# Attention and routed experts on one core: a new order of TensorE's steps in units 0 to 2 of a pair of heads

## The chip, the cores and the metric

One core of a Trainium2 chip runs one program. The metric is the device time of one execution in microseconds (us); several executions are timed and their median is taken. TensorE is called PE in the profile, its weight loads PEld, VectorE DVE, ScalarE ACT, GpSimd POOL and SyncE SP.

## What is computed

Attention over 8 batches, 8 heads, 576 positions and head size 64, with a position bias from a small network; its output feeds a layer of eight experts, of which each token takes one. All of it is float32.

```python
scores = scale * np.matmul(q, k.transpose(0, 1, 3, 2)) + bias
attn = np.exp(scores - np.max(scores, axis=-1, keepdims=True))
attn = attn / (np.sum(attn, axis=-1, keepdims=True) + 1e-09)
x = np.matmul(attn, v)                     # then (token, 512)
e_idx = argmax(x @ w_gate + modality_bias[modality_id]); gate_w = softmax(...)[e_idx]
out[mask] = gate_w[mask, None] * (np.maximum(x[mask] @ w1[e], 0.0) @ w2[e])
```

## The kernel before

There are three stages: the bias table (up to about 66 us in the profiled execution), attention (to about 665 us), and the experts. The change lies in attention.

Attention works through 32 pairs of heads, two heads of one batch at a time, in a loop over n. Each pair has five units u of work, one for each chunk c of 128 rows of scores (the fifth chunk holds the last 64 rows of both heads). The program sets each engine's queue itself: an engine's instructions stand in its queue in the order in which `attention` writes them, and no planner reorders them. The order in a unit is a line of letters in `ORDER`. Work of three pairs is interleaved: scores and exponentials of pair n, products with v of pair n-1, preparation of q and k of pair n+1, loading for pair n+2.

- S (twice a unit) is `scores`, L430: four matmuls of 288 columns (six in unit 4) into one of two score banks `sps`. DVE then adds the bias, writes to `Eb` and takes the minimum `mn` (L445). `e` and `f` are the exponentials on ACT (L459) of the unit's first and second S.
- T and t are `etrans`, parts 1 and 0: four 128x128 transposes each into the bank `eps[1]` or `eps[0]`, which is copied out to `eT`, by ACT or DVE as the list `ON_ACT` says (L315, L317). They belong to the chunk w: in units 0 and 1 to chunks 3 and 4 of pair n-1, in units 2 to 4 to chunks 0 to 2 of pair n. For chunk 4, t is L479 and T is the narrow form, L484: two products of 64 columns, one into each half of the partitions, copied by ACT into the last 64 columns of `rT`.
- R is `rtrans` (L501): four transposes of the left-over columns `rem`, which POOL has copied (C, `compact`), to one of the two small banks `xps`; ACT copies it into `rT`, columns 0 to 511.
- a, A, b, c are `av`, the products with v (L517), for the output's columns 0 to 287 (a then A) and 288 to 575 (b then c). Each is four calls with a 64-column weight that writes one half of the partitions; each call is two matmuls in the profile. A and c end with the remainder (L527, weight `vrem`, moving `rT`), and ACT copies the sum to `xT` (named `xTb` in the profile, L315). The bank is taken in a or b and held in `self.avps`.
- 0, 1, 2, 3, 4 are `prep`: 1 and 0 transpose q (L379), 4 the last rows of q and k (L384), 2 and 3 k (L379), into a small bank, from which DVE or ACT copies into `QT` (L319) or `KT`. W is `swap`, two DMAs on SP's queue (L403, L404) which write `QT` with its halves exchanged; K is `heads`, small DMAs.
- q and k are splits on POOL; L and V are loads on SP's queue; D and Z store and scatter for the routing. X and B are the next step of the routing of the batch before, on PE (X) or elsewhere (B), if one is due; `route_next` picks it. In X are the logits (L771, L794), the ranks (L842) and five transposes of output rows (L866), whose copies to `xrb` ACT does.

The two small banks `xps` are shared by R, X, the products and the preparations. `xbank` hands them out in turn:

```python
def xbank(self):
    self.n_x += 1
    return self.xps[self.n_x % 2]
```

A bank's next writer waits for the copy out of it; the framework places this wait.

Of the kernel before, what the change touches and what calls it, by code (L numbers as in the profile page):

```python
# [22 lines left out]
S = 576  # L23
D = 64
# [43 lines left out]
def n_first(nb):  # L68

    return max(0, min(5, -(-(S * (nb - 2) - E * (TS - 1)) // TS)))  # L70
# [37 lines left out]
class Attn:  # L108
    def __init__(self, tc, io, out, dbg=None):
        self.tc, self.nc, self.io, self.out, self.dbg = tc, tc.nc, io, out, dbg  # L110
        self.B = io["q"].shape[0]
        self.n_tok = self.B * S
        self.n_pair = self.B * NP
        self.K = n_first(self.B)
        self.stores, self.scatters = [], []

# [187 lines left out]
        self.eps = [pp.tile([P, 4, P], F32, name=f"eps{k}") for k in range(2)]  # L304

    def xbank(self):
        self.n_x += 1
        return self.xps[self.n_x % 2]

    ON_ACT = ("av0", "av1", "e00", "e11", "e20", "e30", "e31", "e40", "e41", "prep2", "prep5", "rT", "xr")  # L310
# [193 lines left out]
    def av(self, n, half, part):  # L504

        nc = self.nc
        if half == 0 and part == 0:
            self.xT[n] = self.xTb[n // NP % 2][:, n % NP, :]
        if part == 0:
            self.avps = self.xbank()  # L510
        v = self.vmain[n]
        sl = slice(HS * half, HS * half + HS)
        ps = self.avps[:, 0:HS]
        for k in (0, 1) if part == 0 else (2, 3):
            for h in range(2):
                o = slice(64 * h, 64 * h + 64)
                nc.tensor.matmul(  # L517
                    ps[o, :],
                    v[:, h, k, :],
                    self.eT[:, h, k, sl],  # L520
                    start=k == 0,
                    stop=False,
                    tile_position=(0, 64 * h),
                    skip_group_check=True,
                )
        if part == 1:
            nc.tensor.matmul(ps, self.vrem[n % 2], self.rT[:, sl], start=False, stop=True, skip_group_check=True)  # L527
        if part == 1:
            self.take(f"av{half}", self.xT[n][:, sl], ps)
            if half == 1:  # L530
                del self.vmain[n]

    def first_steps(self, route):
# [40 lines left out]


    ORDER = (
# [5 lines left out]
    )  # L582
# [890 lines left out]
```

## Time and profile before

| what | value |
|---|---|
| median of 3 runs | 1154.85 us (1152.61 to 1155.16) |
| profiled execution, its own time | 1160.33 us |
| its span, first to last instruction | 1158.4 us |
| PE busy | 1121.5 us (97%) |
| DVE busy | 748.6 us (65%) |
| ACT busy | 731.8 us (63%) |
| POOL busy | 361.0 us (31%) |

A share is an average over the three stages, so the attention stage is read by windows. In a row of the timeline stand the start, the length, the engine, the line and the tiles; in square brackets the idle time ahead of it and what ended that. A row of windows has the stretch, its length, the busy time and count of PE, PEld, DVE, ACT and POOL, then the granted clock of PE as a share of full speed, the busy share of the DMA engines and GB/s. Ends of matmuls are modelled, and rows of matmuls in sequence overlap.

### The profile page before, as it was taken

The numbers are of one execution on the slowest core, as the hardware profiler recorded it, in microseconds if no ns is written. First come the engines' busy times: TensorE is split into PE (matmuls) and PEld (weight loads), VectorE is DVE, ScalarE is ACT, GpSimd is POOL, SyncE is SP. The second block draws the span as 40 slices with busy tenths as digits, with TensorE's granted clock in tenths as the row PEclk, the third lists the DMA queues.
The fourth block names the chain that finished last, engine by engine and source line by source line (L and its number), as shares of the span: only waits on it lengthen the run. The fifth ranks groups of instructions, "written<-read, shape, count | busy, mean of one in ns | idle before, by whom it ended". The sixth has DMA issues, their size and how long they took to land. (4 is left out here: it accounts for less than half of the span.)

```text
span 1158.4 us, 23054 instructions
## 1 busy us (share of the span) xinstructions
PE 1121.5 (97%) x8202; PEld 912.4 (79%) x8202; DVE 748.6 (65%) x1556; ACT 731.8 (63%) x1420; POOL 361.0 (31%) x514
## 2 busy tenths in 40 slices
PE   7989999999999999999999999999999999999997
PEld 3457877778777777877777769899999999999975
DVE  8965667676675766756668547584566455645576
ACT  7776767767676676776766646454555455545576
POOL 0013334435434444254352234412112222212122
PEclk9989999999999999999999989999999999999999
DMA  6984434635545544454463721211115115112370
GB/s 176 222 173 113 107 97 124 115 96 130 110 108 121 123 122 104 105 129 108 121 121 96 204 33 56 60 47 46 56 38 175 62 57 196 42 47 65 110 261 26
DMA packets 91456, 124.54 MB, mean 108 GB/s; under 512 B 35713, under 2 KB 60673, under 8 KB 91332
## 3 DMA queue, kind: packets, MB, share of 16 engines
q1 hardware_dynamic: 83236, 101.61, 34.8%
q0 software_dynamic: 8000, 21.35, 6.2%
q8 instruction: 68, 1.11, 0.5%
q14 instruction: 56, 0.46, 0.2%
q10 hardware_dynamic: 96, 0.00, 0.0%
HBM read 140.36 MB, written 19.90 MB: 138 GB/s over the span
## 5 line engine op out<-in xcount | busy, mean ns | idle before, releaser
L445 DVE CUSTOM_DVE_ANT_0 Eb<-sps,NBm 128x576 f32<-128x576 f32 x256 | 189.6, 754 | 160.0 <-PE sps L430 89.1
L459 ACT ACTIVATE Eb<-Eb,mn 128x576 f32<-128x576 f32 x288 | 221.4, 769 | 36.9 <-DVE mn L445 33.5
L430 PE MATMUL sps<-KT,QT 128*128 128x288 f32 x1152 | 220.4, 317 | 3.9 <-DMA QT<-QT 3.7
L430 PEld LDWEIGHTS sps<-KT,QT 128*128 128x128 f32 x1152 | 164.6, 190 | 9.0 <-issue 4.5
L1188 PE MATMUL p<-QT,w1hi 128*128 128x256 f32 x1152 | 162.2, 284 | 0.0
L473 PE MATMUL eps<-idf,Eb 128*128 128x128 f32 x1024 | 158.5, 281 | 0.6 <-DVE lgs L810 0.3
L517 PE MATMUL xps<-eT,vraw 128*64 128x288 f32 x1024 | 155.1, 425 | 1.5 <-DVE QT L1173 1.0
L1188 PEld LDWEIGHTS p<-QT,w1hi 128*128 128x128 f32 x1152 | 149.5, 192 | 2.2 <-ACT w1hi L1161 0.8
L473 PEld LDWEIGHTS eps<-idf,Eb 128*128 128x128 f32 x1024 | 113.9, 141 | 39.0 <-issue 29.3
L1191 DVE SCALAR_TENSOR_TENSOR hl<-p,hh 128x512 fp32r<-128x512 f32 x72 | 49.7, 690 | 141.5 <-ACT hh L1190 140.0
L1214 POOL DMA_INDIRECT out<-mo,idt x36 | 48.0, 1333 | 298.5 <-ACT mo L1213 262.4
L464 POOL COPY rem<-Eb 128x128 f32<-128x128 f32 x128 | 37.2, 291 | 318.8 <-ACT Eb L459 312.3
L1155 DVE TENSOR_TENSOR w2lo<-NBm,w2hi 128x1024 fp32r<-128x1024 f32 x84 | 102.3, 1224 | 24.8 <-ACT w2hi L1154 18.7
L1205 PE MATMUL p<-w2hi,hh 128*128 128x512 f32 x288 | 115.3, 400 | 0.0
L315 ACT ACTIVATE eT<-eps 128x512 f32<-128x512 f32 x192 | 110.6, 591 | 6.8 <-PE eps L473 5.9
L1205 PE MATMUL p<-w2hi,hl 128*128 128x512 f32 x288 | 113.7, 395 | 0.0
L1190 ACT ACTIVATE hh<-p 128x512 fp32r<-128x512 f32 x72 | 43.0, 597 | 111.5 <-PE p L1188 101.3
L315 ACT ACTIVATE xTb<-xps 128x288 f32<-128x288 f32 x64 | 26.3, 411 | 117.0 <-PE xps L527 114.4
L517 PEld LDWEIGHTS xps<-eT,vraw 128*64 128x64 f32 x1024 | 63.2, 138 | 46.1 <-issue 12.3
L1155 DVE TENSOR_TENSOR w1lo<-NBm,w1hi 128x1024 fp32r<-128x1024 f32 x84 | 97.7, 1225 | 0.2 <-ACT w1hi L1154 0.2
L1188 PE MATMUL p<-QT,w1lo 128*128 128x256 f32 x576 | 92.9, 284 | 1.0 <-DVE w1lo L1162 1.0
L1154 ACT CAST w2hi<-NBm 128x1024 fp32r<-128x1024 f32 x84 | 86.8, 1040 | 0.7 <-PEq L1318 0.7
(235 smaller groups left out, 1945.9 us busy)
## 6 DMA issues: line engine op xcount, KB each, us to landing
NBm<-moe_w SPq DMA_DIRECT2D x24, 2048.0 KB
NBm<-moe_w SPq DMA_DIRECT2D x46, 1024.0 KB
QT<-QT SPq DMA_DIRECT2D x64, 304.0 KB
NBm<-xTb SPq DMA_DIRECT2D x32, 288.0 KB
KH<-KT SPq DMA_DIRECT2D x64, 144.0 KB
qraw<-q SPq DMA_DIRECT2D x32, 256.0 KB
kraw<-k SPq DMA_DIRECT2D x32, 256.0 KB
vraw<-v SPq DMA_DIRECT2D x32, 256.0 KB
```

Source lines behind the costliest of these rows:

```text
L315: self.nc.scalar.activation(out, ps, AF.Copy, scale=scale)
L430: nc.tensor.matmul(ps[:, half, :], q, k[:, HS * half : HS * half + HS], start=i == 0, stop=i == len(terms) - 1, skip_group_check=True,)
L445: nc.vector.tensor_tensor_reduce(out=e.rearrange("p (t w) -> p t w", t=2), in0=ps, in1=nb.rearrange("p (t w) -> p t w", t=2), scale=1.0, s ...
L459: self.nc.scalar.activation(e, e, AF.Exp, bias=mn, scale=-1.0, accum_out=sm)
L473: nc.tensor.transpose(ps[:, k, :], e[:, part, P * k : P * k + P], self.idf)
L517: nc.tensor.matmul(ps[o, :], v[:, h, k, :], self.eT[:, h, k, sl], start=k == 0, stop=False, tile_position=(0, 64 * h), skip_group_check=True,)
L1154: self.nc.scalar.copy(h, w)
L1155: self.nc.vector.tensor_tensor(l, w, h.bitcast(F32), op=ALU.subtract)
L1188: nc.tensor.matmul(ps[:, a, :], w[:, c, fs], x[:, c, :], start=i == 0, stop=i == len(ops) - 1)
L1191: nc.vector.scalar_tensor_tensor(hl[:, sl, :], ps, 0.0, hh[:, sl, :].bitcast(F32), op0=ALU.max, op1=ALU.subtract)
L1205: nc.tensor.matmul(ps, h[:, f, sl], m[:, f, :], start=i == 0, stop=i == len(ops) - 1)
L1214: nc.gpsimd.indirect_dma_start(out=self.out, out_offset=IndirectOffsetOnAxis(ap=ids, axis=0), in_=o, in_offset=None, bounds_check=self.n_t ...
```

## The change

Three lines of `ORDER` are rewritten; the last two stay. In unit 0, T and t come between the two S, and R after the second; preparation 0 moves here from unit 1, ahead of a. In unit 1, A comes after the second S, then the narrow T, then b, which moves here from unit 2. Preparation 4 moves from unit 1 to unit 2, ahead of the swap W.

In `av` the remainder of the first half of the columns moves from the end of A to the start of a, and now opens the sum there. In `xbank` a bank that a product still holds is passed over.

```diff
     def xbank(self):
         self.n_x += 1
+        if self.avps is self.xps[self.n_x % 2]:
+            self.n_x += 1
         return self.xps[self.n_x % 2]
...
         ps = self.avps[:, 0:HS]
+        rem = lambda **kw: nc.tensor.matmul(ps, self.vrem[n % 2], self.rT[:, sl], skip_group_check=True, **kw)
+        if half == 0 and part == 0:
+            rem(start=True, stop=False)
         for k in (0, 1) if part == 0 else (2, 3):
...
-                    start=k == 0,
-                    stop=False,
+                    start=half == 1 and k == 0,
+                    stop=half == 0 and k == 3,
...
         if part == 1:
-            nc.tensor.matmul(ps, self.vrem[n % 2], self.rT[:, sl], start=False, stop=True, skip_group_check=True)
-        if part == 1:
+            if half == 1:
+                rem(start=False, stop=True)
             self.take(f"av{half}", self.xT[n][:, sl], ps)
+            self.avps = None
...
     ORDER = (
-        "S R S e f X T a t B C Z",
-        "L D S 1 A t e S 4 f 0 C T",
-        "t S W S e f b q C Z T",
+        "S T t S R e f X 0 a B C Z",
+        "L D S 1 t e S f C A T b",
+        "t S 4 W S e f q C Z T",
         "B S c e S T 3 2 t f C V",
         "S K k X X e T B X t D",
     )
```

More of the change, by code (lines that the diff above doesn't have):

```diff
@@ L526, in av @@
         if part == 1:
-            nc.tensor.matmul(ps, self.vrem[n % 2], self.rT[:, sl], start=False, stop=True, skip_group_check=True)
-        if part == 1:
+            if half == 1:
+                rem(start=False, stop=True)
             self.take(f"av{half}", self.xT[n][:, sl], ps)
+            self.avps = None
             if half == 1:
```

## The prediction

> **What bounds the kernel now.** I read the busy shares on the page first, then the windows over the attention stage (90 to 665 us), then the waits of TensorE there, then the timeline of a few pairs of heads.
>
> ```profile
> PE 1121.5 (97%) x8202; PEld 912.4 (79%) x8202; DVE 748.6 (65%) x1556; ACT 731.8 (63%) x1420; POOL 361.0 (31%) x514
> 300.00:400.00 100.00, 99.31 (x790) 78.09 (x787) 65.99 (x173) 69.40 (x165) 42.25 (x71) 1.00 0.51 115
> PE xps L866 <- DVE base L847: 2.1, 7, 0.3
> ```
>
> TensorE (PE) is busy 99.31 of 100 us, DVE 66, ACT 69. The third row is the longest of PE's waits between 90 and 660 us: 2.1 us in all. So PE waits for practically nobody, and its queue sets the end. A change here is worth the PE time it saves, less every wait that it opens on PE. The next rows are the timeline (start, length, engine, line): L430 scores, L473 and L501 transposes, L379 and L384 preparations, L484 narrow transposes, L517 products with v, L527 their remainder.
>
> ```profile
> 306.54 0.60 PE L501 MATMUL xps<-idf,rem 128*128 128x128 f32 x4
> 306.90 0.77 PE L430 MATMUL sps<-KT,QT 128*128 128x288 f32 x4
> 307.18 0.60 ACT L315 ACTIVATE rT<-xps 128x512 f32<-128x512 f32 x1 [0.37 <-PE xps L501]
> 308.66 0.78 ACT L459 ACTIVATE Eb<-Eb,mn 128x576 f32<-128x576 f32 x1 [0.89 <-DVE mn L445]
> 312.02 0.69 DVE L319 TENSOR_SCALAR QT<-xps 128x512 fp32r<-128x512 f32 x1
> 313.45 0.78 PE L430 MATMUL sps<-KT,QT 128*128 128x288 f32 x4
> 314.07 0.22 PE L384 MATMUL xps<-idr,qs 128*128 128x128 f32 x1
> 314.19 0.51 PE L379 MATMUL xps<-idr,qs 128*128 128x128 f32 x4
> 314.63 0.34 PE L484 MATMUL eps<-idf,Eb 128*64 128x64 f32 x4
> 315.98 0.48 SPq L403 DMA_DIRECT2D QT<-QT  x1
> 316.22 0.76 DVE L445 CUSTOM_DVE_ANT_0 Eb<-sps,NBm 128x576 f32<-128x576 f32 x1 [0.27 <-issue]
> 316.54 1.19 PE L517 MATMUL xps<-eT,vraw 128*64 128x288 f32 x8
> 316.90 0.75 DVE L445 CUSTOM_DVE_ANT_0 Eb<-sps,NBm 128x576 f32<-128x576 f32 x1
> 317.67 0.66 PE L473 MATMUL eps<-idf,Eb 128*128 128x128 f32 x4
> 318.08 0.77 PE L430 MATMUL sps<-KT,QT 128*128 128x288 f32 x4
> 318.78 1.19 PE L517 MATMUL xps<-eT,vraw 128*64 128x288 f32 x8
> 319.90 0.75 PE L527 MATMUL xps<-rT,vrem 128*128 128x288 f32 x2
> 320.28 0.91 PE L430 MATMUL sps<-KT,QT 128*128 128x288 f32 x4
> 320.69 0.41 ACT L315 ACTIVATE xTb<-xps 128x288 f32<-128x288 f32 x1 [2.04 <-PE xps L527]
> 321.03 0.60 PE L473 MATMUL eps<-idf,Eb 128*128 128x128 f32 x4
> 321.22 0.76 DVE L445 CUSTOM_DVE_ANT_0 Eb<-sps,NBm 128x576 f32<-128x576 f32 x1 [1.43 <-PE sps L430]
> ```
>
> PE rows overlap in their modelled ends, so I price PE by the distance from one start to the next.
>
> **Part 1, what PE saves.** Products and narrow transposes use half the array's columns (the form 128*64). Going in: scores take 0.62 before a full-width group (313.45 to 314.07), 0.70 before products (318.08 to 318.78): 0.08. Coming out: the last pair of the eight products starts 1.19 - 0.41 (a group's two-matmul tail is 0.41 long) = 0.78 after the first, three steps of 0.26; with the fourth, 1.04; the next group starts after 1.13 (316.54 to 317.67): 0.09. That next group of transposes then takes 0.41 (317.67 to 318.08) where after scores it takes 0.35 (321.03 to the next group at 321.38): 0.06. The first half-width weights must be loaded too; no row parts that off, I take 0.06 like the full-width ones. One excursion costs 0.29. Before, a pair has five: a, A, the narrow T, b, c. After, A, T and b are one, and a and c remain: two fewer, 2 x 0.29 x 32 pairs = **18.6 us saved**. Bounds: 0, if T beside the products still costs a change, and 22 at 0.35 each (a remainder behind products pays 0.11: 319.90 to 321.03 is 1.13, against 0.48 for its four passes plus 0.62 - and one of its two moves ahead of a). No matmul is added or dropped.
> By the Trainium skill ("TensorEngine Tiling (Array Packing)", Overview, Key Properties), changing the tiling mode drains the array, and another tile in the same mode does not. That is the saving; no run here has yet shown narrow transposes beside products, and without the rule this part would be worth 0 to 18.6.
>
> **Part 2, b waits behind ACT.** There are two small PSUM banks, taken in turn. In unit 1 the order is now "t e S f C A T b": a took one bank, preparation 1 the other, so b gets a's bank back, and must wait until ACT has copied A's result out. That such a third user waits is seen in pair 0, where preparation 0 waits for preparation 1's copy:
>
> ```profile
> 72.99 0.69 DVE L319 TENSOR_SCALAR QT<-xps 128x512 fp32r<-128x512 f32 x1
> 73.73 0.40 PEld L379 LDWEIGHTS xps<-idr,qs 128*128 128x128 f32 x4 [0.58 <-DVE QT L319]
> 304.33 0.76 DVE L445 CUSTOM_DVE_ANT_0 Eb<-sps,NBr 128x576 f32<-128x576 f32 x1 [0.17 <-ACT Eb L459]
> 305.13 0.78 ACT L459 ACTIVATE Eb<-Eb,mn 128x576 f32<-128x576 f32 x1 [0.84 <-DVE mn L445]
> ```
>
> The copy ends 73.68, PE goes on 0.05 later. Queues run in the written order, and the copy of A stands in ACT's queue behind f, the exponential of the second scores. So, from the end of those scores' row: DVE starts 0.03 later (321.19 to 321.22); f starts 0.80 after that (304.33 to 305.13); f holds ACT 0.78; the copy 0.41; 0.05 to PE: 2.07. DVE is 0.07 late besides, since one reduction (0.68, 316.22 to 316.90) and preparation 1's copy (0.69) stand ahead, 1.37 against 1.30 that PE needs from the first scores to the second (0.62, preparation 0.33, transposes 0.35). PE itself is ready for b 0.70 + 1.04 + T (0.34 row less its 0.22 tail, and a step of 0.05: 0.17) = 1.91 after those scores start, 1.13 after their row ends (0.78). Wait: 2.14 - 1.13 = **1.0 us**, 31 pairs: 31; in the last, without scores, only the copy: 0.3. Sum 31.3. Before, b came in unit 2, eight groups of PE work after A, and the copy stood ahead of both exponentials. Behind b all of PE's queue waits, unit 2's scores first. Bounds 0.85 (DVE on time, a drain of 0.1 before T) to 1.2.
>
> **Part 3, a's remainder comes first.** It reads rT, which ACT copies after R. R's row ends 307.14, the copy starts 307.18 and lasts 0.60; with 0.05, PE may go 0.69 after that end. Between stands only preparation 0: R takes 0.36 to the next start (306.54 to 306.90), preparation 0 some 0.38 (314.19 to 314.63 is 0.44 with a drain); PE is ready 0.14 after R's row end. Wait **0.55**, in 25 pairs: 13.8. Bounds 0.4 to 0.7. In the seven pairs whose X in unit 0 transposes rows (L866), the two banks go R, X, 0, a: so 0 waits for rT, and a for X's copy, which ACT does after e and f.
>
> ```profile
> 345.39 0.60 PE L866 MATMUL xps<-idf,xTb 128*128 128x128 f32 x4
> 347.87 0.60 ACT L315 ACTIVATE xrb<-xps 128x512 f32<-128x512 f32 x1 [0.55 <-DMA xg<-xrb]
> ```
>
> From R's end: 0.64 + 2 x 0.78 + 0.60 + 0.05 = 2.85; PE is ready at 0.14 + 0.36 = 0.50. Wait 2.35, x7 = 16.5 (bounds 1.8 to 2.5). The DMA in that row is no further delay: it let go 2.48 after X's start, and X's copy now comes 2.44 after a start that is itself 0.9 later (T, t against R, 0.88).
>
> **Part 4, t in unit 0** now follows T at once and needs the bank that the last transposes of unit 4 filled.
>
> ```profile
> 119.62 0.78 PE L430 MATMUL sps<-KT,QT 128*128 128x288 f32 x4
> 120.75 0.58 ACT L315 ACTIVATE eT<-eps 128x512 f32<-128x512 f32 x1
> 362.60 0.78 PE L430 MATMUL sps<-KT,QT 128*128 128x288 f32 x4
> 363.35 0.58 ACT L315 ACTIVATE eT<-eps 128x512 f32<-128x512 f32 x1
> ```
>
> It is free 1.71 and 1.33 after the unit's first scores start, plus 0.05; t is ready at 0.62 + 0.44 = 1.06. Waits 0.70 (three early pairs, before any routing) and 0.32 (six, one batch's first pair): 4.0. Bounds 0 and 9.
>
> **Part 5, what costs nothing.** SP's swap of q now stands behind preparation 4 in unit 2.
>
> ```profile
> 316.00:320.30 4.30, 4.30 (x32) 2.65 (x30) 2.81 (x7) 2.65 (x8) 2.56 (x4) 1.00 0.68 149
> 320.30:320.90 0.60, 0.60 (x6) 0.55 (x5) 0.00 (x0) 0.21 (x1) 0.00 (x0) 1.00 0.04 14
> ```
>
> It is issued at 315.98 and the DMA falls silent at 320.3 (0.04 busy). The next pair needs it 18.7 us after this pair's first scores, near 324.7: 4.4 spare. The issue comes about 1 us later in its unit, and b (1.13 and a drain) no longer lies behind it: 2.2 spent, 2.2 left. Without that cover each us late is a us on PE, in 31 pairs. Preparation 0 in unit 0 has its q split two units before; POOL's next split waits for preparation 4, early in the same unit: 0.
>
> **Part 6, the clock.** Windows of busy time, the granted clock after POOL's count:
>
> ```profile
> 644.25:647.66 3.41, 2.19 (x17) 1.75 (x16) 1.60 (x8) 2.35 (x5) 2.34 (x4) 1.00 1.04 234
> 647.66:651.07 3.41, 3.41 (x29) 2.61 (x28) 1.53 (x4) 2.22 (x5) 0.00 (x0) 1.00 0.60 161
> 664.73:668.14 3.41, 1.66 (x12) 0.98 (x10) 0.44 (x2) 2.48 (x6) 2.50 (x5) 1.00 0.01 0
> 668.14:671.55 3.41, 2.81 (x11) 1.46 (x12) 0.54 (x1) 0.79 (x2) 2.94 (x4) 0.50 0.62 126
> ```
>
> After a slice with 1.75 us idle the next ran at half speed; after one with 1.22 idle (644.25) it ran at full speed. Seven waits of 2.35 lie between, depending on where the slices cut. I take half of them, 1.7 us lost each: 6. Bounds 0 and 24 (each, two slices).
> The Trainium skill ("TensorE: Matmul & The Clock Gate", Why this matters for your kernels) warns of gaps over about 3 us alone. By it the 6 would be 0; the row after 664.73 speaks against that.
>
> **Sum.** -18.6 + 31.3 + 13.8 + 16.5 + 4.0 + 6 = +53.0. The profiled execution took 1160.3 (span 1158.4): 1213. The median is 1154.85, 0.5% under it: **1208 us**.
>
> **Rivals.** *Faster, 1136:* the copies reach PE in time and the 18.6 alone is left. It decides where a pair's waits fall under 0.58; part 2 alone is over that by its lowest bound, and ACT's 69% is no argument, since what counts is its order, not its load. 0.05. *Milder, 1182:* all low bounds (22 saved, 26.7, 10, 12.6, 0, 0): +27. 0.09. *The clock drops at every long wait, for two slices:* 6 becomes 24, 1226; the slice of 644.25 speaks against its reaching b's waits too. 0.11. *The change doesn't do what it says:* T beside the products still costs both drains, the waits remain: +72, 1227. 0.04. The forecast has 0.69, and no balance at zero 0.02.
>
> So faster 0.05, same 0.02, slower 0.93; 0.2% (2.3 us) is about what this kernel's measurement can tell from none. The range 1180 to 1232 takes in milder and both slower rivals.
>
> **What would show it.** New rows among PE's waits: products on ACT's copy xTb, some 31 us in 31; the remainder L527 on rT, near 14, and seven of 2 us on xrb; transposes on eT, 4. T directly beside L517 without the steps of 0.08 and 0.09. PE's busy share near 93%; attention ending near 718 instead of 665; the stage behind it as long as now. Wrong it would be if b started within 0.3 us of T.

## The result, and the profile after

The changed kernel takes **1220.8 us** (median of 4, 1216.08 to 1221.5); the kernel before took 1154.52 beside it. The ratio is 1.056, 95% interval 1.0526 to 1.0594. The profiled execution took 1221.32 us, its span 1219.4.

In the new file a line up to some 510 stands 4 further down and a later one 8 or 9: scores L434, transposes L477 and L483, narrow transposes L488, R L505, the remainder L519, products L525, preparations L383 and L388, copies L319 (ACT) and L321, L323 (DVE). The busy row of the page after:

```profile
PE 1127.8 (92%) x8202; PEld 918.2 (75%) x8202; DVE 749.7 (61%) x1556; ACT 732.6 (60%) x1420; POOL 361.1 (30%) x514
```

The work is the same; each engine has about the busy time that it had. What grew is idle time of PE. The windows after, the hundred us shown before and then four pairs (one batch) that no slower clock touches:

```profile
300.00:400.00 100.00, 91.26 (x706) 72.02 (x705) 59.06 (x151) 64.12 (x154) 40.66 (x64) 0.98 0.40 99
399.21:482.21 83.00, 75.05 (x589) 58.84 (x588) 50.18 (x130) 52.98 (x127) 32.49 (x53) 1.00 0.43 104
```

The same four pairs before, from the same R to the same R:

```profile
363.22:437.92 74.70, 74.36 (x589) 58.60 (x588) 48.98 (x130) 53.06 (x127) 32.12 (x53) 1.00 0.50 116
```

589 matmul records in 75.05 us against 589 in 74.36: PE is idle 7.95 us per batch instead of 0.34, and the batch takes 8.30 longer. The rows of R (line L505 after, then L501 before; shortest, median and longest in ns, then the first and the last start in us) show that the whole loss lies in attention:

```profile
L505 PE MATMUL xps<-idf,rem x128: 270/272/421, 86.1 to 732.2; 128*128 128x128 f32 x128
```

```profile
L501 PE MATMUL xps<-idf,rem x128: 270/272/332, 83.9 to 667.0; 128*128 128x128 f32 x128
```

From the first R to the last pass 646.1 us instead of 583.1: +63.0, where the whole span grew by 61.0. What PE waits for in attention after, as us in all, number of waits and the longest (of these rows only the last and, with 0.3 us, lgs were there before):

```profile
PE xps L525 <- ACT xTb L319: 28.1, 30, 1.0
PE xps L519 <- ACT xrb L319: 8.8, 6, 1.5
PE eps L477 <- DVE lgs L819: 7.0, 7, 1.2
PE xps L519 <- ACT rT L319: 6.1, 16, 0.4
PE xps L383 <- ACT rT L319: 4.6, 13, 0.4
...
PE xps L519 <- DVE lt L321: 1.4, 1, 1.4
...
PE sps L434 <- DMA QT<-QT: 0.6, 1, 0.6
```

The list counts idle time behind the modelled end of the row before, so I measure a wait, as the prediction did, by the distance from one start to the next against the same two steps where nothing is waited for. Steps of a pair with rows of X, and then of one without:

```profile
206.39 0.60 PE L875 MATMUL xps<-idf,xTb 128*128 128x128 f32 x4
...
207.24 0.53 PE L383 MATMUL xps<-idr,qs 128*128 128x128 f32 x4 [0.25 <-ACT rT L319]
...
209.24 0.87 PE L519 MATMUL xps<-rT,vrem 128*128 128x288 f32 x2 [1.46 <-ACT xrb L319]
...
314.82 0.60 PE L505 MATMUL xps<-idf,rem 128*128 128x128 f32 x4
315.18 0.54 PE L383 MATMUL xps<-idr,qs 128*128 128x128 f32 x4
315.46 0.60 ACT L319 ACTIVATE rT<-xps 128x512 f32<-128x512 f32 x1 [0.37 <-PE xps L505]
316.11 0.75 PE L519 MATMUL xps<-rT,vrem 128*128 128x288 f32 x2 [0.39 <-ACT rT L319]
...
319.22 0.77 PE L434 MATMUL sps<-KT,QT 128*128 128x288 f32 x4
...
320.14 0.76 DVE L449 CUSTOM_DVE_ANT_0 Eb<-sps,NBm 128x576 f32<-128x576 f32 x1
...
320.94 0.78 ACT L463 ACTIVATE Eb<-Eb,mn 128x576 f32<-128x576 f32 x1
320.94 0.28 PE L488 MATMUL eps<-idf,Eb 128*64 128x64 f32 x4
...
321.72 0.39 ACT L319 ACTIVATE xTb<-xps 128x288 f32<-128x288 f32 x1
...
322.16 1.19 PE L525 MATMUL xps<-eT,vraw 128*64 128x288 f32 x8 [0.93 <-ACT xTb L319]
```

In the pair with X, preparation 0 comes 0.85 after X (0.44 there before), and the remainder 2.00 after preparation 0 (0.38 where nothing waits). In the other, the remainder comes 0.93 after preparation 0, since rT is copied from 315.46 to 316.06. The rows from 319.22 on are the chain of Part 2, link by link: scores at 319.22, DVE at 320.14, the exponential f at 320.94, the copy of A at 321.72, b at 322.16. From the narrow transposes to b pass 1.22 us; 0.11 would do (e2).

The new order thus moves the end by 5.6%, with no matmul added. In us, the distances over all pairs add up to: b 33.6; the remainder behind rT 13.5 (the remainder is 0.55 late, or in the seven pairs with logits in X the preparation 0.51); the product behind X 14.1 (2.0 in six pairs with rows of X, 0.4 in the last such pair, and 1.6 in a late pair with logits, the row lt); T behind the routing 7.9; other waits of t and T about 5; the clock about 7.8; the shorter layout -10. That is 72. In the order before, the step behind R's scores waited for the routing (it came 1.12 or 0.83 after these scores instead of 0.61); that wait is gone there and gives back 5. The balance closes to about 4 of the 63.

### The profile page after: what moved, and what is told of

It reads as the page before. It is cut to its first block, busy times and chain, and to the rows that moved or that the text cites. A ratio compares the mean times of both kernels' runs of the same rounds, so it can differ in the third digit from the quotient of the medians.

```text
span 1219.4 us, 22971 instructions
## 1 busy us (share of the span) xinstructions
PE 1127.8 (92%) x8202; PEld 918.2 (75%) x8202; DVE 749.7 (61%) x1556; ACT 732.6 (60%) x1420; POOL 361.1 (30%) x514
## 4 chain that ended last, share of the span: by engine, by line
PE 69%; DMA 9%; DVE 7%; issue 7%; ACT 7%; POOL 0%; SPq 0%; POOLq 0%; DVEq 0%; ACTq 0%
PE p L1197 13%; PE p L1214 12%; PE sps L434 12%; PE xps L525 9%; PE eps L477 8%; DVE Eb L449 4%; PE xps L519 4%; ACT Eb L463 3%; PE bps L196 3%; DMA NBr<-xg,idt 3%; PE xps L383 2%; ACT rT L319 1%; DMA out<-mo,idt 1%; PE xps L505 1%; DMA NBm<-xTb 1%
## 5 line engine op out<-in xcount | busy, mean ns | idle before, releaser
L434 PE MATMUL sps<-KT,QT 128*128 128x288 f32 x1152 | 230.4, 323 | 3.1 <-DMA QT<-QT 3.0
L319 ACT ACTIVATE eT<-eps 128x512 f32<-128x512 f32 x192 | 111.6, 593 | 152.0 <-PE eps L483 78.7
L434 PEld LDWEIGHTS sps<-KT,QT 128*128 128x128 f32 x1152 | 167.9, 192 | 25.7 <-issue 16.4
L525 PE MATMUL xps<-eT,vraw 128*64 128x288 f32 x1024 | 155.9, 427 | 28.5 <-ACT xTb L319 28.5
L477 PE MATMUL eps<-idf,Eb 128*128 128x128 f32 x1024 | 151.9, 277 | 8.1 <-DVE lgs L819 7.0
L477 PEld LDWEIGHTS eps<-idf,Eb 128*128 128x128 f32 x1024 | 116.4, 141 | 33.7 <-issue 16.0
L525 PEld LDWEIGHTS xps<-eT,vraw 128*64 128x64 f32 x1024 | 63.1, 138 | 81.9 <-ACT xTb L319 32.8
L1163 ACT CAST w1hi<-NBm 128x1024 fp32r<-128x1024 f32 x84 | 81.9, 1051 | 0.0
```

Source lines behind the costliest of these rows:

```text
L319: self.nc.scalar.activation(out, ps, AF.Copy, scale=scale)
L434: nc.tensor.matmul(ps[:, half, :], q, k[:, HS * half : HS * half + HS], start=i == 0, stop=i == len(terms) - 1, skip_group_check=True,)
L477: nc.tensor.transpose(ps[:, k, :], e[:, part, P * k : P * k + P], self.idf)
L525: nc.tensor.matmul(ps[o, :], v[:, h, k, :], self.eT[:, h, k, sl], start=half == 1 and k == 0, stop=half == 0 and k == 3, tile_position=(0, ...
L1163: self.nc.scalar.copy(h, w)
```

## The experiments

e1 to e5 and e9 are edits of the changed kernel, e6 and e8 of e5; e7 is the changed kernel with the old order. Letters are those of `ORDER`. "Less" is against the median of the changed kernel, 1220.8.

**e1: ACT's copy of A ahead of f.** PE's steps stay as they are; only f moves behind A in the writing, and so in ACT's queue.

```diff
-        "L D S 1 t e S f C A T b",
+        "L D S 1 t e S A f C T b",
```

> The changed kernel with one step moved in unit 1: A stands ahead of f and C, so TensorE's order is the same and ACT copies A's result before the second exponential. Theory (b waits because the copy of A stands behind f in ACT's queue): only the copy itself is left to wait for, 0.04 + 0.41 + 0.05 less the 0.12 to 0.17 of the narrow T, some 0.35 instead of 1.07 in each pair: 23 us less than the changed kernel's 1220.8, about 1198; PE's wait for xTb falls from 28 us to under 10. Rival 1 (b waits for DVE's late scores or for its own data, the order in ACT's queue does not matter): within 3 us of 1221. Rival 2 (the delay is the price of the array's layouts, the waits only show where it comes out): within 3 us of 1221, the wait row replaced by another.

Measured: 1204.2 us, ratio 1.042 (1.0384 to 1.0456); 16.6 us less. The timeline of e1 around one b:

```profile
315.81 0.28 PE L488 MATMUL eps<-idf,Eb 128*64 128x64 f32 x4
316.02 0.41 ACT L319 ACTIVATE xTb<-xps 128x288 f32<-128x288 f32 x1 [0.31 <-PE xps L525]
316.33 0.77 ACT L463 ACTIVATE Eb<-Eb,mn 128x576 f32<-128x576 f32 x1
316.48 0.68 PEld L525 LDWEIGHTS xps<-eT,vraw 128*64 128x64 f32 x8 [0.53 <-ACT xTb L319]
```

b now stands 0.67 behind the narrow transposes instead of 1.22: 0.55 x 31 = 17.1 us, about what the time lost. So f in front of the copy was half of the wait. PE's row for xTb fell from 28.1 to 12.3 us, not to under 10 as expected. What is left is the copy itself: A's row ends only 0.17 after the narrow transposes start (0.04 to the copy, 0.41, 0.05 to PE), about 0.56 where I had expected 0.35.

**e2: b takes the bank that a did not have.**

```diff
         if part == 0:
             self.avps = self.xbank()
+            if half == 1 and self.avps is self.av0:
+                self.avps = None
+                self.avps = self.xbank()
+            self.av0 = self.avps
```

> The changed kernel, but b takes the small bank that a did not have (the one of preparation 1). Theory (it is the shared bank that makes b wait): no wait for xTb is left at all, 31 x 1.07 and 0.05 a pair for weights loaded ahead: 35 us less, about 1186. Rival 1 (b waits for its data, eT of the last chunk): no change, 1221. Rival 2 (the wait moves on to preparation 4, which now takes a's bank): less than 10 us gained, above 1210, with a new row for L388.

Measured: 1181.44 us, ratio 1.0224 (1.0187 to 1.0262); 39.4 less than the changed kernel. In e2's timeline (products now L529) b follows at once:

```profile
327.46 0.28 PE L488 MATMUL eps<-idf,Eb 128*64 128x64 f32 x4
327.51 0.69 PEld L529 LDWEIGHTS xps<-eT,vraw 128*64 128x64 f32 x8
327.57 1.14 PE L529 MATMUL xps<-eT,vraw 128*64 128x288 f32 x8
```

0.11 from the narrow transposes to b, with no drain, and its weights are loaded ahead. PE's row for xTb is gone, so the wait was wholly a matter of the bank, and it is the largest single cause. The 39.4 are more than the 33.6 of the wait: b itself is 0.05 shorter to the next start, and in this run two slices of attention behind the first R run at half speed instead of five. Against that, waits for SP's swap of q grow to 4.5 us. This split is worked out from the trace; no run parts it.

**e3: R first in unit 0,** so that rT is copied long before the remainder reads it.

```diff
-        "S T t S R e f X 0 a B C Z",
+        "S R T t S e f X 0 a B C Z",
```

> The changed kernel with R ahead of T, t and the second scores in unit 0 (S R T t S ...). Theory (the remainder waits for rT because R comes last): the wait of 0.55 goes in the pairs without rows in X, some 24 x 0.55 = 13, and T and t come 0.36 later against the copies that they wait for, some 6 more: 19 less, about 1202; the seven pairs with rows in X keep waits near 1.6, and the clock still drops there. Rival (the remainder waits for another thing than rT, such as its weights or the bank that the preparation uses): under 8 less, above 1213.

Measured: 1205.58 us, ratio 1.0426 (1.0385 to 1.0466); 15.2 less. PE's waits of e3:

```profile
PE xps L525 <- ACT xTb L319: 31.3, 30, 1.4
PE xps L519 <- ACT xrb L319: 13.4, 6, 3.5
PE eps L477 <- DVE lgs L819: 4.1, 7, 0.8
PE sps L434 <- DMA QT<-QT: 3.6, 2, 2.2
...
PE xps L519 <- ACT rT L319: 0.6, 1, 0.6
```

The waits for rT are gone, as expected (13.5 by distances); the row lgs is shorter by 2.9 because T comes 0.35 later. Some of it is given back, so that 15.2 came of the 19 expected: the product behind X's rows waits 4.6 longer, b 3.2 longer, and the waits for SP's swap of q, which the changed kernel had once, for 0.6, come to 3.6.

**e4: X behind a,** so that the banks no longer go R, X, 0, a.

```diff
-        "S T t S R e f X 0 a B C Z",
+        "S T t S R e f 0 a X B C Z",
```

> The changed kernel with X in unit 0 after a instead of ahead of preparation 0 and a. Theory (in seven pairs a waits for the copy of X's rows behind both exponentials, and these waits are what makes the clock drop): the waits there fall from 2.1 to 0.55, 7 x 1.55 = 11, and five or six stretches at half speed go with them, 1.6 each: 19 less, about 1202, clock 1.00 through the attention stage but its start. Rival 1 (the clock drops for the many short waits): 11 less, about 1210, and half-speed stretches as many as before. Rival 2 (preparation 1 now waits for X's copy instead): within 4 of 1221.

Measured: 1204.42 us, ratio 1.0419 (1.0383 to 1.0455); 16.4 less. No product waits for xrb any more, and the granted clock over attention is full:

```profile
PE xps L519 <- ACT rT L319: 12.9, 31, 0.8
...
PE xps L383 <- ACT xrb L319: 1.5, 6, 0.5
```

```profile
90.00:700.00 610.00, 558.09 (x4361) 437.31 (x4360) 375.20 (x990) 395.45 (x940) 231.05 (x373) 1.00 0.44 108
```

The 14.1 us of these waits and 7.8 of slow clock go; the seven pairs then wait for rT like the others (7 x 0.55 = 3.9), and preparation 1 for X's copy (1.5). 21.9 - 5.4 = 16.5, about the time measured. The short waits of b are all still there (29.0 us in 32), so it was not they that lowered the clock.

**e9: T and t of unit 0 behind the second scores,** for the row lgs, which the prediction did not have.

```diff
-        "S T t S R e f X 0 a B C Z",
+        "S S t T R e f X 0 a B C Z",
```

> The changed kernel, with T and t of unit 0 moved behind the second scores instead of between the two. Nothing else is moved, so the waits of b, of the remainder and of the product behind X's rows stay. Theory (T waits for DVE's copy out of eps[1], which stands behind the routing's logits on DVE, 7.0 us in seven pairs, and t 0.3 to 0.7 us in nine): T comes 0.62 us later, so the row of transposes behind lgs falls to under 2 us and that of eT under 1; time 7 us less, about 1213. Rival (that row is only the last of several things that T waits for, or the copy is later still): the row stays above 4 us and the time within 3 us of the changed kernel's.

Measured: 1211.92 us, ratio 1.0493 (1.0466 to 1.0521); 8.9 less in time, 7.9 in span. In e9's waits lgs has no row, and eT is left with:

```profile
PE eps L477 <- ACT eT L319: 1.9, 4, 0.7
```

eT is over the bound of 1 that I had given; the rest holds. What T waits for stands in the timeline of the changed kernel:

```profile
182.18 0.55 DVE L804 TENSOR_TENSOR lw<-xps,rec 128x256 f32<-128x256 f32 x2
182.76 0.77 DVE L812 TENSOR_REDUCE lgs<-lw 128x40 f32<-128x320 f32 x1
183.44 0.69 DVE L321 COPY eT<-eps 128x512 f32<-128x512 f32 x1
184.03 0.20 DVE L819 TENSOR_TENSOR lgs<-lgs,mbias 128x40 f32<-128x40 f32 x1
184.27 1.06 PE L477 MATMUL eps<-idf,Eb 128*128 128x128 f32 x8 [0.96 <-DVE lgs L819]
```

The row names L819, but that is only the last thing that DVE did. T needs the bank `eps[1]`, and DVE's copy out of it (183.44 to 184.13) stands behind two steps of the routing of the batch before. T starts 0.15 after the end of this copy, and so it does in the pair at 123.75, where no routing runs.

**e5: all repairs at once** (R first, t and T behind the second scores and X behind a in unit 0; f behind A; b's bank as in e2, whose lines are not shown again). The question is what the shorter layout is worth once nothing waits.

```diff
-        "S T t S R e f X 0 a B C Z",
-        "L D S 1 t e S f C A T b",
+        "S R S t T e f 0 a X B C Z",
+        "L D S 1 t e S A f C T b",
```

> All three cures at once on the changed kernel: unit 0 is S R S t T e f 0 a X, A stands ahead of f in unit 1, and b takes the bank that a did not have. Theory (the layout gain is real and was buried under the waits): no wait of PE on xTb, rT, xrb or lgs is left above 1 us in total each; a pair without routing takes 16.9 instead of 17.4 us of the kernel before, 0.44 x 32 = 14 less than before: about 1141. Rival 1 (fewer excursions save nothing, the rest of the order costs): within 3 us of before, 1155. Rival 2 (a new wait: preparation 1 on X's copy, or the swap landing late): 1145 to 1155, with the row named in PE's waits.

Measured: **1147.03 us** (1144.04 to 1149.43), ratio 0.9934 (0.9914 to 0.9953): faster than both kernels, 0.66% under the one before. Four pairs of e5, and its longest row among PE's waits:

```profile
285.88:359.07 73.19, 72.72 (x590) 58.39 (x588) 50.10 (x130) 52.98 (x127) 32.55 (x53) 1.00 0.48 118
```

```profile
PE sps L434 <- DMA QT<-QT: 8.5, 4, 3.0
```

Such a batch took 75.22 (288.00 to 363.22) and 74.70 (363.22 to 437.92) before and takes 73.19 here, 0.4 to 0.5 us a pair; over the whole stage 8.5 us are given back in four waits for the swap of q, which is Rival 2. Not all of the gain is the layout's. In a pair where neither order waits, the first of this batch, it is 0.36 (18.17 against 18.53), less than the 0.44 expected; in early pairs without routing, where transposes still come 0.19 late, 0.18 (17.19 and 17.21 against 17.38). The second and third pair of the batch also lose the routing waits that the order before had behind R.

**e6: one excursion more.** e5, but A in front of the second scores of unit 1, so that A stands alone and T and b together.

```diff
-        "L D S 1 t e S A f C T b",
+        "L D S 1 t e A S f C T b",
```

> The combined kernel with one more excursion and nothing else: A stands ahead of the second scores in unit 1, so that scores part it from the narrow T and b. Theory (an excursion to the half-width layout costs 0.29): 32 x 0.29 = 9 more than the combined kernel, about 1150. Rival (going in and out is hidden or free): within 2 us of the combined kernel. Rival 2 (the price is 0.14, the drains alone): 4.5 more.

Measured: 1157.46 us, ratio 1.0029 (1.0013 to 1.0045), 10.4 more than e5. Four pairs of e6:

```profile
288.36:362.94 74.58, 74.12 (x590) 58.13 (x589) 50.34 (x130) 52.71 (x127) 32.55 (x53) 1.00 0.47 116
```

1.39 more in four pairs: 0.35 us for one excursion into half the columns and back, where Part 1 had 0.29 and 0.35 as its upper end. It is the price at this place: here the excursion goes in behind transposes (t takes 0.56 to the next start instead of 0.38 in e5), and Part 1 had read 0.08 behind scores.

**e7: the remainder first, and nothing else.** The order of the kernel before, with the new `av` and `xbank`.

> The kernel before with one part of the change alone: the remainder of the first half opens the sum in a instead of closing it in A; the order of the units is that of before. Theory (this part moves work between places of the same kind, the number of excursions stays five, rT is long there because two scores and T stand between): within 2 us of before. Rival (the place of the remainder is itself what costs, for its weights cannot be loaded ahead): 0.11 to 0.2 a pair, 3.5 to 6 us slower than before.

Measured: 1154.67 us, ratio 1.0001 (0.9986 to 1.0015). Moving the remainder costs and brings nothing where rT is ready; in the early pairs without routing, where it still waits for rT, a pair takes 17.66 instead of 17.38. With e7, the order alone is left as the cause of the change's 5.6%.

**e8: the swap of q issued earlier,** for e5's waits of 8.5 us.

```diff
-        "t S 4 W S e f q C Z T",
+        "4 W t S S e f q C Z T",
```

> The combined kernel with preparation 4 and the swap W at the very start of unit 2 (4 W t S S ...), so that the two DMAs of the swap are issued some 1.7 us earlier (transposes 0.41, scores 0.61 and a DVE reduction 0.7 no longer stand ahead). Theory (part 5 was wrong in a few pairs: the swap, issued later and followed by less work, lands late where loads and stores share the queue; PE's row for QT shows 8.5 us in 4 waits): that row falls to 3 us or less, and the time by 5 to 6, about 1141. Rival (the swap waits for the DMA queue's other transfers, not for its issue): the row stays, within 2 us of 1147.

Measured: 1150.52 us, ratio 0.995 (0.9932 to 0.9968): no gain on e5, though 3.5 above it where the rival had said within 2. The wait did not go away: 7.3 us in two waits, against 8.5 in four. Two rows of e8's timeline on SP's queue, then PE, around its longest one, and a window behind the swap's issue:

```profile
214.78 3.23 SPq L337 DMA_DIRECT2D qraw<-q  x1
...
222.16 0.54 SPq L407 DMA_DIRECT2D QT<-QT  x1
...
233.25 0.82 PE L434 MATMUL sps<-KT,QT 128*128 128x288 f32 x2 [4.79 <-DMA QT<-QT]
...
222.00:224.00 2.00, 2.00 (x15) 1.46 (x12) 0.73 (x3) 0.97 (x4) 0.00 (x0) 1.00 0.50 6
```

The swap was issued 11 us before the scores that need it, and still came 4.8 too late; a load ahead of it took 3.23 to issue, where such an issue mostly takes about 0.6. So the theory of a late issue falls. In the 2 us after the issue the DMA engines are busy for half of the time and move only 6 GB/s, so transfers already on the way are slow there; that the swap waits for these is likely and not shown, and why they are slow is open.

## Why the prediction was right, point by point

The forecast was +53 in the profiled execution, where +61 came (1160.33 to 1221.32), and 1208 us for the median, where 1220.8 came: the profiled execution before lay 0.5% over its median, and the one after lies at it. The direction and the mechanism stand; two terms were mis-sized or missing. By its steps:

- **Part 1, the saving:** the sign is right, the size is not: 18.6 predicted. By distances, a pair without routing takes 17.38 before and about 17.07 after once its waits are taken off: 0.3 a pair, 10 us. Part 1 took one price, 0.29, for every excursion; what one costs depends on its neighbours. e6 gives 0.35 for one behind transposes. (The Trainium skill, "TensorEngine Tiling (Array Packing)", Key Properties, says that a change of the tiling mode drains the array and gives no price; 0.35 in e6 and 0.11 without a change in e2 agree with it.) Where A, T and b were joined, the distances shrink by less: A 1.02 instead of 1.12, preparation 0 ahead of the next step 0.38 instead of 0.43 ahead of T, T 0.11 (in e2) instead of 0.27, and nothing on the way into b, since the two scores ahead of b took 1.23 before, twice 0.61. That is 0.31 a pair where 0.58 had been taken; the other distances of the pair about cancel out. e5 agrees with it: 0.36 in a pair where nothing waits, 0.05 of it for the weights of b. The split is read from the distances; no run parts it. "T beside the products still costs a change" (the rival at 1227) is wrong: 0.11 in e2.
- **Part 2, b behind ACT:** 31.3 predicted, 33.6 measured (1.08 a pair). e1 shows that the place in ACT's queue makes half of it, e2 that the bank makes all of it.
- **Part 3, remainder:** 13.8 predicted, 13.5 measured; e3 removes it. X's rows: 16.5 predicted, 14.1 measured, and e4 removes it. It is 2.0 instead of 2.35 a pair, in six pairs and not in seven; 1.6 of the 14.1 lie in a pair with logits that the prediction did not count.
- **Part 4, T and t:** this is the step that failed. It asked only when t's bank is free, 4.0 us, and about 5 came. It did not ask it of T, whose bank DVE frees, and the routing stands in DVE's queue in one pair of each batch: 1.13 x 7 = 7.9 us more. e9 shows it. The trace before had the sign of it: in the pair whose R starts at 174.89, T comes 0.83 after the scores instead of 0.61, again 0.15 behind this copy.
- **Part 5, nothing:** right for the changed kernel (0.6 us for the swap, once). But the swap is waited for in other runs, 3.6 us in e3, 4.5 in e2 and 8.5 in e5, and in the order before 1.3. By e8 the place of its issue is not the cause, so whether the 2.2 us spare were reckoned rightly is open.
- **Part 6, the clock:** 6 predicted, about 7.8 measured: behind the first R five slices ran at half speed, four of them after pairs with X's rows and one after the pair with the wait for lt; about 1.55 us lost each, an estimate from the distances there.

So the sum's two errors are Part 1, 9 us too much saved, and T's wait, 8 us that no term had. Both made the forecast too low. That it missed by no more is in part luck: the 5 us of waits for the routing that the order before had behind R, which the prediction left out too, go the other way. The milder case (1182) had b at 0.85, which the runs exclude, and "faster" needed waits under 0.58 a pair, where b alone has 1.08.

## What to carry to other kernels

When steps of the bounding engine are put side by side, count the buffers that they share: with two banks taken in turn, the third user waits for the first one's copy, and that copy comes when its engine's queue gets to it, however idle that engine is on average (ACT 60%). Ask this of every bank whose next writer moves, and look for other work, such as a routing step every fourth pair, in the queue of the engine that frees it. Then repair the waits one by one: the same joining of A, T and b, 5.6% slower as first written, is 0.66% faster with another bank and a few letters moved.

## What the runs showed of the hardware

In these traces the granted clock falls to 0.50 for slices of 3.41 us, and it goes with the sum of PE's idle time in a slice rather than with the longest gap. A slice of the changed kernel and the next, and the same of e9, each with a wait of 1.46 us for X's copy:

```profile
206.34:209.75 3.41, 1.70 (x12) 1.11 (x10) 1.27 (x3) 2.59 (x6) 1.32 (x3) 1.00 0.63 214
209.75:213.16 3.41, 3.41 (x13) 1.78 (x13) 0.00 (x0) 0.00 (x0) 2.09 (x4) 0.50 0.61 192
...
455.32:458.73 3.41, 1.93 (x12) 1.17 (x14) 0.69 (x1) 1.96 (x5) 1.37 (x3) 1.00 0.67 206
458.73:462.15 3.42, 3.42 (x28) 2.48 (x26) 2.04 (x5) 1.35 (x3) 1.06 (x2) 1.00 0.49 157
```

In the changed kernel a second wait of 0.25 falls into the slice, 1.71 us are idle in all, and the next slice runs at 0.50. In e9 the earlier wait falls ahead of the slice, 1.48 are idle, and the next runs at full speed. Part 6's rows agree: 1.22 idle, full speed next; 1.75, half. The Trainium skill ("TensorE: Matmul & The Clock Gate", Why this matters for your kernels) warns of gaps of over about 3 us; here two waits of 0.25 and 1.46 us in one slice were enough, so the measurement decides. The idle time alone is no sharp rule either: in the experts' stage of e6 a slice with 1.93 us idle was followed by full speed.

```profile
721.46:724.87 3.41, 1.48 (x9) 1.30 (x10) 2.47 (x4) 1.20 (x3) 2.10 (x3) 1.00 0.15 57
724.87:728.29 3.42, 3.42 (x17) 2.81 (x16) 0.00 (x0) 0.00 (x0) 2.14 (x3) 1.00 0.27 98
```

While b waits for its bank, its weights are not loaded either: in e1 b's loads start with b, at 316.48, in e2 0.06 before it, and b then takes 1.12 and 1.07 to the next start.
